# Attention, routed experts and a dense layer in one kernel: one group's preparation a chunk later, a gate split in two, and two small moves

## The chip, the cores and the metric

The kernel runs on one core of a Trainium2 chip. The metric is the device time of one execution in microseconds (us). A core has TensorE (PE in the profile, with its weight loads as PEld), VectorE (DVE), ScalarE (ACT), GpSimd (POOL) and SyncE (SP), which issues most of the DMAs. Each engine takes its own instructions strictly in their order, and waits on semaphores for the others.

## The reference

Three layers in a row, all in float32, on 2304 tokens of width 512:

```
scores = scale * q @ k.T          # 4 x 8 heads, 576 positions, 64 wide
scores = where(0 <= i - j < 64, scores, -1e9);  x = softmax(scores) @ v
logits = x @ w_gate + log1p(exp(x @ w_noise)) * noise
top2   = the two best of 8 experts;  weights = softmax over those two
out[t] = sum over the two of  weight * (relu(x[t] @ w1[e]) @ w2[e])      # 512 -> 1024 -> 512
h = out @ w_in                                                          # 512 -> 2048
g = h if h >= 1;  0 if h <= -1;  else (h + 1)**2 / 4
result = g @ w_out                                                      # 2048 -> 512
```

## The kernel before

The work is one instruction stream per engine, in an order that the program writes out by hand: there is no planner, so an instruction stands where the Python code emits it. Every float32 matrix product is done as three products of rounded parts (high by high, low by high, high by low), so each activation and each weight is split into a high part (a copy on ACT into the rounded type) and a low part (a subtraction on DVE).

The stages around the change, in order of time:

- **Expert 0.** Attention ends; the tokens of expert 0 are worked as unit `0a` (three blocks of 128 rows) and unit `0b` (two). Each unit runs over 8 chunks of the hidden width: `mm1` makes 128 hidden columns for all rows, `act_relu` (lines 892 to 897) takes them out of PSUM as high part (ACT) and low part (DVE), both in the tile `hall`, and `mm2` multiplies them by the second weights. `mm1` of the next chunk is emitted before `mm2` of this one. While `0a` runs, the rest of the routing (`tail`) is fed in as a Python generator, one piece at each `more()`, twice per chunk: once ahead of `mm1`, once behind it. `count` (line 811) is a part of it: it sorts the experts by load and fills `rank_i`, the tables by which the later experts gather their rows, with two products and two reductions on DVE (lines 841 and 845).
- **Expert 1** has six blocks, the sixth of 64 rows. During `0b` each block is gathered, transposed by TensorE into a PSUM bank, and taken out by ACT (high) and DVE (low) in `xpose`. All six blocks use the same bank, number 7 (`TR`), and the last two are turned at the same place of the program, ahead of the last-but-one `mm2` of `0b`.
- **The dense layer** comes after expert 7, whose last unit is `7b`. Its first group of rows, `g0` (two blocks, 256 rows), is worked plainly: 8 chunks `p`, each with two gate halves `f`, in `plain(ui, p)`. For each `f`, 12 matmuls fill bank 0 or 1 (in turn), and `act_gate` computes the piecewise square: ACT reads the bank (`r`), ACT halves it (`m`), two DVE instructions, ACT writes the high part and DVE the low part into `hall`. Then come the 12 matmuls of `mm2`: six of `f=0`, six of `f=1`; of each three the last one reads the low part.
- **The second group**, `g1` (four blocks), and the ones behind it use a Winograd-like scheme with seven products for eight, from `wino(ui, p)`. Its rows have to be ready before that: for each block the two expert results are loaded from DRAM (`y`, on the POOL queue, behind the scatters of unit `7b` into the same DRAM tensor), mixed by the routing weights (`mix_two`, ACT then DVE), turned by TensorE (`xturn`), copied by ACT (`xcopy`), combined (`xsums`, DVE), and split into high and low (`split_two`). All that is placed in the chunks of `g0`: by the table `FILL` into the middle of a gate, and by conditions in the last loop behind a seventh of an `mm2`. `plain(p + 1)` is emitted at the start of step `p`, ahead of that step's `mm2`. At step 6 the first `wino` of `g1` is interleaved with the `mm2` of `g0`; its seven products use bank 0 and bank 1 in turn, and the first one is taken out by ACT (`sg`).

Of the kernel before, what the change touches and what calls it, by code (L numbers as in the profile page):

```python
# [31 lines left out]
NB = 5  # L32
# [25 lines left out]
def fused_kernel(ctx, tc, qT, kT, v, wg, noise, wcat, out, wd=None):  # L58
# [734 lines left out]
    def tail():  # L793
        while live or oq or pq:
            place()
            advance(TAIL)
            yield
        finish_ids([(NA, NB), (0, NA), (NB, E * JB)])
        prep_gather(units[1], 0)
        count()  # L800
        rte.close()
        pool["xp"] = xpc.enter_context(tc.tile_pool(name="xp", bufs=1, reuse_waits="tile", side="right"))
        for n in range(NF, NF + 2):
            load_raw(n)
        yield
        for b in range(1, units[1]["nb"]):
            prep_gather(units[1], b)
            yield
        prep_gather(units[2], 0)

    def count():
        cnt = bank[6][:, CNT:CNT + E]
        nc.tensor.matmul(cnt, lhsT=ones, rhs=state["C"], start=True, stop=True)


        cn = gp.tile([P, E], F32, tag="cn", name="cn")
        key = gp.tile([P, E], F32, tag="key", name="key")
        nc.vector.tensor_scalar(out=cn, in0=cnt, scalar1=16.0, scalar2=None, op0=ALU.mult)
        nc.vector.tensor_tensor(out=key, in0=cn, in1=io8, op=ALU.add)
        nc.vector.memset(key[:, 0:1], -1.0)  # L820
        c8 = gp.tile([P, E], F32, tag="c8", name="c8")
        i8 = gp.tile([P, E], U32, tag="i8", name="i8")
        nc.vector.max(out=c8, in_=key)
        nc.vector.max_index(out=i8, in_max=c8, in_values=key)
        nc.vector.tensor_scalar(out=cnt_i[:, 1:1 + E], in0=i8, scalar1=float(NF), scalar2=None, op0=ALU.mult)
        tf = gp.tile([P, E], F32, tag="tf", name="tf")
        nc.vector.tensor_copy(tf, i8)
        nc.vector.tensor_copy(c8[:, E - 1:E], cn[:, 0:1])
        nc.vector.tensor_tensor(out=c8, in0=c8, in1=caps, op=ALU.subtract)
        nc.vector.tensor_tensor(out=c8[:, 0:E - 1], in0=c8[:, 0:E - 1], in1=tf[:, 0:E - 1], op=ALU.subtract)  # L830
        m1 = gp.tile([P, 1], F32, tag="m1", name="m1")
        nc.vector.tensor_reduce(out=m1, in_=c8, axis=AX.X, op=ALU.max)
        nc.vector.tensor_scalar(out=cnt_i[:, 0:1], in0=m1, scalar1=0.0, scalar2=None, op0=ALU.max)
        R, J = E - 1, NB + 1
        o = gp.tile([P, R, E], F32, tag="to", name="to")
        nc.vector.tensor_tensor(out=o, in0=io8.unsqueeze(1).to_broadcast([P, R, E]),
                                in1=tf[:, 0:R].unsqueeze(2).to_broadcast([P, R, E]), op=ALU.is_equal)
        for a, src in enumerate((src_i, dst_i)):
            f = wk.tile([P, 512], F32, tag="pt", name=f"rk{a}", bufs=PTB)[:, 0:R * J * E]
            f = f.rearrange("p (r j e) -> p r j e", j=J, e=E)  # L840
            nc.vector.tensor_tensor(
                out=f, in0=o.unsqueeze(2).to_broadcast([P, R, J, E]),
                in1=src.rearrange("p (e j) -> p j e", j=JB)[:, 0:J, :].unsqueeze(1).to_broadcast([P, R, J, E]),
                op=ALU.mult)
            nc.vector.tensor_reduce(out=rank_i[:, a], in_=f, axis=AX.X, op=ALU.max)
# [46 lines left out]
    def act_relu(ps, hh, hl, w):  # L892
        nc.scalar.activation(hh, ps, AF.Relu)  # L893
        for o, t in hl:
            c = slice(o, o + t.shape[1])
            nc.vector.scalar_tensor_tensor(out=t, in0=ps[:, c], scalar=0.0, in1=hh[:, c].bitcast(F32), op0=ALU.max,  # L896
                                           op1=ALU.subtract)

    def act_gate(ps, hh, hl, w):
        (_, hl), = hl  # L900
        r = pool["sc"].tile([P, 512], F32, tag="s", name="r")[:, 0:w]
        m = pool["sc"].tile([P, 512], F32, tag="s", name="m")[:, 0:w]
        nc.scalar.activation(r, ps, AF.Relu, bias=1.0)  # L903
        nc.scalar.activation(m, r, AF.Copy, scale=0.5)  # L904
        nc.vector.scalar_tensor_tensor(out=r, in0=m, scalar=1.0, in1=r, op0=ALU.min, op1=ALU.subtract)  # L905
        nc.vector.scalar_tensor_tensor(out=r, in0=m, scalar=1.0, in1=r, op0=ALU.min, op1=ALU.mult)  # L906
        for x in parts_of:
            next(x)
        nc.scalar.activation(hh, r, AF.Copy, scale=-1.0)  # L909
        nc.vector.scalar_tensor_tensor(out=hl, in0=r, scalar=-1.0, in1=hh.bitcast(F32), op0=ALU.mult, op1=ALU.subtract)  # L910
        for x in parts_of:
            next(x, None)
        parts_of.clear()
# [203 lines left out]
    def plain(ui, p):  # L1117
        w = wi[p % WS]
        for f in range(2):
            n = N2 + 2 * p + f  # L1120

            def part(h):
                return [w[:, 2 * f + k // 2, h, P * (k % 2):P * (k % 2) + P] for k in range(4)]
            key = units[ui]["key"]
            parts_of.extend(x() for x in FILL.get((p, f), ()))
            mm1_of(key, n, units[ui]["T"], act_gate, units[ui]["m1"], part(0), part(1))
        load_in(p + WS)

    xops, cs, hs = {}, {}, {}
# [125 lines left out]
        for _ in split_two(ui, j):  # L1255
            pass

    def copy_two(ui, b):
        xcopy(ui, b)
        yield  # L1260

    def sums_two(ui, part):
        yield
        xsums(ui, part)


    SPLITS = {0: [int(F0 <= f < F0 + NF - EW) for f in range(NF)], 1: [0] + [1] * (NF - 1),
              U7A: [1] + [0] * (NF - 1)}
# [12 lines left out]
    for s in range(len(seq)):  # L1281
# [41 lines left out]
        def ahead_xpose():  # L1323
            for x, b, w in ahead:
                if f == (turn_at[b] if ui == WIDE - 1 else w + 2):
                    prep_xpose(x, b, bank[0] if ui == WIDE else TR)
        for x, b, w in ahead:
            if f == w + 1 and x["e"] is None:
                fill.append(lambda x=x, b=b: prep_mix(x, b))
# [45 lines left out]
        if ui == U7B and f:  # L1375
# [3 lines left out]
    assert ndec == n64 and nsplit == nload == N2  # L1379

    AT = ({(4, 0): (None,), (4, 4): (0,), (4, 5): (1,), (5, 0): (2,), (5, 1): (3,), (5, 3): (4,), (6, 2): (5,), (6, 3): (6,)},
          {(5, 3): (6,)})
    g1 = FIRST2 + 1

    def later(fn, *a):
        return lambda: fn(*a)
    FILL.update({(2, 1): [later(mix_two, units[g1], b) for b in (0, 1)],
                 (3, 0): [later(mix_two, units[g1], b) for b in (2, 3)],
                 (4, 0): [later(split_two, g1, 0), later(split_two, g1, 1)],
                 (4, 1): [later(sums_two, g1, (0, 1))],  # L1390
                 (5, 0): [later(sums_two, g1, (2, 3))],
                 (5, 1): [later(split_two, g1, j) for j in (2, 3)],
                 (6, 0): [later(split_two, g1, j) for j in (4, 5)]})
    ndone = 1
    for q, (ui, p) in enumerate(items):
        if q == 0:
# [21 lines left out]
        for j in range(7):  # L1418
            if nxt:
# [6 lines left out]
                if not late:  # L1426
                    if 1 <= p < 3 and j in (2, 4):
                        prep_mix(nxt, 2 * (p - 1) + j // 2 - 1)
                    if 2 <= p < 4 and j in (1, 3):
                        xturn(ui + 1, 2 * (p - 2) + j // 2)  # L1430
                        xcopy(ui + 1, 2 * (p - 2) + j // 2)
                elif p == 2:
                    if j in (0, 1, 5, 6):
                        xturn(ui + 1, j if j < 2 else j - 3)
                    for b in {3: (0, 1), 6: (2, 3)}.get(j, ()):
                        xcopy(ui + 1, b)
                for x in AT[late].get((p, j), ()):
                    xsums(ui + 1) if x is None else xsplit(ui + 1, x)
            if j < len(g):
# [38 lines left out]
```

## Time and profile before

| what | value |
|---|---|
| time, median of 3 runs (range) | 971.39 us (968.99 to 973.98) |
| time of the profiled execution | 971.69 us |
| its span, first to last instruction | 969.9 us |
| TensorE busy | 944.0 us (97%) |
| VectorE / ScalarE / GpSimd busy | 661.6 / 447.5 / 220.2 us |
| mean granted clock of TensorE | 0.994 of full speed |

The profiled execution is 0.3 us above the median. TensorE is busy nearly all the time, so a change can gain only where TensorE stands still or runs at its lower clock; the other engines have idle time of their own that costs nothing.

### The profile page before, as it was taken

How to read it: one execution, taken by the hardware profiler on the slowest of the kernel's cores; microseconds unless marked ns; L12 is line 12 of the kernel's file. 1: busy time of each engine (PE TensorE's matmuls, PEld its weight loads, DVE VectorE, ACT ScalarE, POOL GpSimd, SP SyncE). 2: the span in 40 equal slices, each digit the busy share in tenths (PEclk: the TensorE clock that was granted, in tenths of full speed). 3: DMA queues.
4: the chain of work that ended last, by engine and by line, in shares of the span. 5: the costliest groups of instructions: out<-in, count | busy, mean ns of one | idle time of the engine just before them, and what ended most of it. 6: DMA issues, size and time to landing. Idle time of an engine off the chain costs nothing. (4 is left out here: it accounts for less than half of the span.)

```text
span 969.9 us, 18052 instructions
## 1 busy us (share of the span) xinstructions
PE 944.0 (97%) x6781; PEld 834.8 (86%) x6781; DVE 661.6 (68%) x1388; ACT 447.5 (46%) x920; POOL 220.2 (23%) x273
## 2 busy tenths in 40 slices
PE   8998999999999999999999997999999999999998
PEld 6886878988898989889888886898999889889897
DVE  4689565378997968889543365766766677577664
ACT  6897324345555555555432355334334333443222
POOL 3221113132634354254402130013002201300000
PEclk9999999999999999999999998999999999999999
DMA  8874125445878878757727574684576558546531
GB/s 249 296 266 144 56 97 187 178 167 192 291 257 290 260 244 278 254 196 251 252 82 239 178 234 159 200 298 155 174 249 230 173 174 295 165 161 214 189 106 44
DMA packets 91274, 196.95 MB, mean 203 GB/s; under 512 B 7320, under 2 KB 18072, under 8 KB 91184
## 3 DMA queue, kind: packets, MB, share of 16 engines
q1 hardware_dynamic: 83152, 171.68, 53.6%
q0 software_dynamic: 6736, 21.86, 6.3%
q10 hardware_dynamic: 1296, 2.23, 0.6%
q8 instruction: 54, 0.88, 0.4%
q14 instruction: 36, 0.29, 0.1%
HBM read 155.45 MB, written 40.29 MB: 202 GB/s over the span
## 5 line engine op out<-in xcount | busy, mean ns | idle before, releaser
L949 PE MATMUL bank<-wo,hall 128*128 128x512 f32 x864 | 239.5, 396 | 0.0
L949 PE MATMUL bank<-w,hall 128*128 128x512 f32 (+3 forms) x944 | 236.0, 398 | 1.4 <-DVE hall L896 1.3
L949 PEld LDWEIGHTS bank<-w,hall 128*128 128x128 f32 (+3 forms) x944 | 168.4, 184 | 37.0 <-DVE hall L896 1.7
L949 PEld LDWEIGHTS bank<-wo,hall 128*128 128x128 f32 x864 | 147.8, 190 | 17.5
L893 ACT ACTIVATE hall<-bank 128x288 fp32r<-128x288 f32 (+6 forms) x128 | 54.0, 422 | 223.3 <-PE bank L885 204.1
L885 PE MATMUL bank<-xhie,w 128*128 128x288 f32 (+4 forms) x768 | 123.0, 302 | 1.6 <-DVE hall L896 1.5
L885 PEld LDWEIGHTS bank<-xhie,w 128*128 128x128 f32 x768 | 113.9, 189 | 9.1 <-DVE hall L896 3.4
L896 DVE SCALAR_TENSOR_TENSOR hall<-bank,hall 128x288 fp32r<-128x288 f32 (+7 forms) x168 | 59.8, 391 | 87.2 <-ACT hall L893 78.5
L149 DVE TENSOR_TENSOR w<-raw,w 128x1024 fp32r<-128x1024 f32 (+1 forms) x71 | 82.4, 1160 | 24.4 <-ACT w L158 20.5
L1163 PEld LDWEIGHTS bank<-xb,wi 128*128 128x128 f32 x576 | 80.4, 188 | 11.5 <-DVE wg L1148 1.2
L1187 ACT ACTIVATE hall<-cg 128x512 fp32r<-128x512 f32 x64 | 40.3, 629 | 100.5 <-DVE cg L1185 100.5
L1163 PE MATMUL bank<-xb,wi 128*128 128x256 f32 x576 | 84.8, 283 | 1.8 <-ACT r L903 0.8
L1163 PEld LDWEIGHTS bank<-xc,wi 128*128 128x128 f32 x480 | 67.2, 188 | 7.6 <-DVE wg L1148 0.6
L1030 POOL TENSOR_TENSOR y<-y,y 128x512 f32<-128x512 f32 x14 | 19.1, 1363 | 227.2 <-ACT y L1029 227.2
L1163 PE MATMUL bank<-xc,wi 128*128 128x256 f32 x480 | 70.2, 281 | 0.2
L158 ACT ACTIVATE w<-raw 128x1024 fp32r<-128x1024 f32 (+1 forms) x71 | 69.3, 976 | 0.0
L885 PE MATMUL bank<-xloe,w 128*128 128x288 f32 (+4 forms) x384 | 69.0, 301 | 0.0
L204 POOL TENSOR_TENSOR td<-rawd 128x512 f32<-128x512 f32 x32 | 33.3, 1039 | 140.7 <-DVE rawd L202 78.2
L1181 ACT ACTIVATE mg<-cg 128x512 f32<-128x512 f32 x64 | 40.1, 626 | 47.1 <-DVE cg L1153 45.4
L1182 DVE SCALAR_TENSOR_TENSOR cg<-mg,cg 128x512 f32<-128x512 f32 x64 | 47.0, 734 | 18.8 <-ACT mg L1181 18.8
L885 PEld LDWEIGHTS bank<-xloe,w 128*128 128x128 f32 x384 | 58.0, 188 | 0.0
L1191 DVE SCALAR_TENSOR_TENSOR hall<-cg,hall 128x512 fp32r<-128x512 f32 x64 | 45.9, 718 | 9.1 <-ACT hall L1187 8.7
(279 smaller groups left out, 1443.5 us busy)
## 6 DMA issues: line engine op xcount, KB each, us to landing
wi<-w1o SPq DMA_DIRECT2D x56, 1024.0 KB
raw<-wcat SPq DMA_DIRECT2D x64, 512.0 KB
rawd<-wd SPq DMA_DIRECT2D x32, 512.0 KB
w1o<-so SPq DMA_DIRECT2D x64, 256.0 KB
y<-y_dram SPq DMA_DIRECT2D x28, 256.0 KB
vE<-v SPq DMA_DIRECT2D x18, 260.0 KB
x_dram<-x SPq DMA_DIRECT2D x18, 256.0 KB
k<-kT SPq DMA_DIRECT2D x8, 512.0 KB
```

The lines of the kernel that those rows point to most:

```text
L149: nc.vector.tensor_tensor(out=w[:, 1, c], in0=t[:, c], in1=w[:, 0, c].bitcast(F32), op=ALU.subtract)
L158: nc.scalar.activation(w[:, 0, c], t[:, c], AF.Copy)
L204: nc.gpsimd.tensor_tensor(out=t, in0=hf, in1=lf, op=ALU.add)
L885: nc.tensor.matmul(ps, lhsT=l[k], rhs=r[:, k, s:s + w], start=(c == 0), stop=(c == len(prods) - 1))
L893: nc.scalar.activation(hh, ps, AF.Relu)
L896: nc.vector.scalar_tensor_tensor(out=t, in0=ps[:, c], scalar=0.0, in1=hh[:, c].bitcast(F32), op0=ALU.max, op1=ALU.subtract)
L949: nc.tensor.matmul(M2[b][0:w], lhsT=h2[:, o:o + w], rhs=r[n], start=(first and a == 0), stop=(last and a == end))
L1163: nc.tensor.matmul(ps, lhsT=w[:, l, k * P:k * P + P], rhs=r[:, m, k, :], start=(c == 0), stop=(c == len(prods) - 1))
L1181: nc.scalar.activation(st["m"], c, AF.Relu, scale=0.5)
L1182: nc.vector.scalar_tensor_tensor(out=c, in0=st["m"], scalar=1.0, in1=c, op0=ALU.min, op1=ALU.subtract)
L1187: nc.scalar.activation(h2[:, 0:T], c, AF.Copy, scale=-1.0)
L1191: nc.vector.scalar_tensor_tensor(out=h2[:, T:2 * T], in0=c, scalar=-1.0, in1=h2[:, 0:T].bitcast(F32), op0=ALU.mult, op1=ALU.subtract)
```

## The change

Five edits:

1. `count` gets a `yield` ahead of the two rank tables, and `tail` passes it on with `yield from`, so that the tables and what follows are emitted one `more()` later.
2. `act_gate` no longer finishes its own gate. It keeps `(r, hh, hl)` in `held_gate`, and the next gate finishes it (`close_gate`) right behind its own read of the bank. The last gate is closed at the end of the last `plain`.
3. The sixth block of expert 1 is turned into bank 4 instead of bank 7.
4. The preparation of `g1` moves back: the mixing of blocks 0 and 1 by one gate or two, the turns from step 2 to steps 3 and 4, copies, sums and splits accordingly. The sums leave the gate and stand in step 4; the last split goes into the last plain chunk.
5. Two helpers that are no longer used are removed.

```
-        count()
+        yield from count()
...
+        yield
         for a, src in enumerate((src_i, dst_i)):
...
+    held_gate = []
+
+    def close_gate():
+        for r, hh, hl in held_gate:
+            nc.scalar.activation(hh, r, AF.Copy, scale=-1.0)
+            nc.vector.scalar_tensor_tensor(out=hl, in0=r, scalar=-1.0, in1=hh.bitcast(F32), op0=ALU.mult,
+                                           op1=ALU.subtract)
+        held_gate.clear()
+
     def act_gate(ps, hh, hl, w):
...
         nc.scalar.activation(r, ps, AF.Relu, bias=1.0)
+        close_gate()
         nc.scalar.activation(m, r, AF.Copy, scale=0.5)
...
+        held_gate.append((r, hh, hl))
         for x in parts_of:
             next(x)
-        nc.scalar.activation(hh, r, AF.Copy, scale=-1.0)
-        nc.vector.scalar_tensor_tensor(out=hl, in0=r, scalar=-1.0, in1=hh.bitcast(F32), op0=ALU.mult, op1=ALU.subtract)
...
+        if p == NPR - 1:
+            close_gate()
...
-                    prep_xpose(x, b, bank[0] if ui == WIDE else TR)
+                    prep_xpose(x, b, bank[0] if ui == WIDE else bank[4] if ui == WIDE - 1 and b == NB else TR)
...
-          {(5, 3): (6,)})
+          {})
+    TURN, COPY = {(3, 0): (0,), (3, 1): (1,), (3, 6): (2,), (4, 0): (3,)}, {(3, 3): (0, 1), (4, 2): (2, 3)}
...
-    FILL.update({(2, 1): [later(mix_two, units[g1], b) for b in (0, 1)],
-                 (3, 0): [later(mix_two, units[g1], b) for b in (2, 3)],
-                 (4, 0): [later(split_two, g1, 0), later(split_two, g1, 1)],
-                 (4, 1): [later(sums_two, g1, (0, 1))],
-                 (5, 0): [later(sums_two, g1, (2, 3))],
-                 (5, 1): [later(split_two, g1, j) for j in (2, 3)],
-                 (6, 0): [later(split_two, g1, j) for j in (4, 5)]})
+    FILL.update({(3, 0): [later(mix_two, units[g1], 0)],
+                 (3, 1): [later(mix_two, units[g1], 1)],
+                 (4, 0): [later(mix_two, units[g1], b) for b in (2, 3)],
+                 (5, 0): [later(split_two, g1, j) for j in (0, 1)],
+                 (6, 0): [later(split_two, g1, j) for j in (2, 3)],
+                 (6, 1): [later(split_two, g1, j) for j in (4, 5)],
+                 (7, 0): [later(split_two, g1, 6)]})
...
-                elif p == 2:
-                    if j in (0, 1, 5, 6):
-                        xturn(ui + 1, j if j < 2 else j - 3)
-                    for b in {3: (0, 1), 6: (2, 3)}.get(j, ()):
+                else:
+                    for b in TURN.get((p, j), ()):
+                        xturn(ui + 1, b)
+                    for b in COPY.get((p, j), ()):
                         xcopy(ui + 1, b)
+                    if p == 4 and j > 4:
+                        xsums(ui + 1, (0, 1) if j == 5 else (2, 3))
```

On **VectorE, at the end of expert 0's unit `0a`**, this stands in a row before (`rk` and `rank_i` are the rank tables, `hall` the low parts of the ReLUs of the last two chunks of `0a`):

```order
L833 TENSOR_SCALAR cnt_i_194<-m1_2437 128x1
L836 TENSOR_TENSOR to_2440<-io8_177,tf_2432 128x56
L841 TENSOR_TENSOR rk0_2442<-to_2440,src_i_190 128x336
L845 TENSOR_REDUCE rank_i_205<-rk0_2442 128x42
L841 TENSOR_TENSOR rk1_2445<-to_2440,dst_i_191 128x336
L845 TENSOR_REDUCE rank_i_205<-rk1_2445 128x42
L896 SCALAR_TENSOR_TENSOR hall_2150<-bank1_74,hall_2150 128x384
L896 SCALAR_TENSOR_TENSOR hall_2150<-bank2_75,hall_2150 128x384
```

And in the changed kernel, on VectorE at the same place:

```order
L833 TENSOR_SCALAR cnt_i_194<-m1_2437 128x1
L836 TENSOR_TENSOR to_2440<-io8_177,tf_2432 128x56
L842 TENSOR_TENSOR rk0_2451<-to_2440,src_i_190 128x336
L846 TENSOR_REDUCE rank_i_205<-rk0_2451 128x42
L842 TENSOR_TENSOR rk1_2454<-to_2440,dst_i_191 128x336
L846 TENSOR_REDUCE rank_i_205<-rk1_2454 128x42
L897 SCALAR_TENSOR_TENSOR hall_2150<-bank1_74,hall_2150 128x384
L897 SCALAR_TENSOR_TENSOR hall_2150<-bank2_75,hall_2150 128x384
```

Nothing moved there: only the line numbers and a tile's number differ.

On **ScalarE, in the gates of `g0` around the mixing** (`r` and `m` as above, `hall` the high part of a gate, `y2` to `y5` the four blocks of `g1`), before, from the second half of `plain(2)` to the second half of `plain(3)`:

```order
L903 ACTIVATE r_7017<-bank1_74 128x256
L904 ACTIVATE m_7018<-r_7017 128x256
L1019 ACTIVATE y2_6963<-y2_6963,wts_189 128x512
L1019 ACTIVATE y3_6966<-y3_6966,wts_189 128x512
L909 ACTIVATE hall_2150<-r_7017 128x256
L903 ACTIVATE r_7056<-bank0_73 128x256
L904 ACTIVATE m_7057<-r_7056 128x256
L1019 ACTIVATE y4_6970<-y4_6970,wts_189 128x512
L1019 ACTIVATE y5_0_6974<-y5_0_6974,wts_189 128x512
L909 ACTIVATE hall_2150<-r_7056 128x256
```

And now, on ScalarE, from the first half of `plain(3)` to the first half of `plain(4)`:

```order
L913 ACTIVATE r_7050<-bank0_73 128x256
L904 ACTIVATE hall_2150<-r_7015 128x256
L915 ACTIVATE m_7051<-r_7050 128x256
L1029 ACTIVATE y2_6961<-y2_6961,wts_189 128x512
L913 ACTIVATE r_7072<-bank1_74 128x256
L904 ACTIVATE hall_2150<-r_7050 128x256
L915 ACTIVATE m_7073<-r_7072 128x256
L1029 ACTIVATE y3_6964<-y3_6964,wts_189 128x512
L913 ACTIVATE r_7109<-bank0_73 128x256
L904 ACTIVATE hall_2150<-r_7072 128x256
L915 ACTIVATE m_7110<-r_7109 128x256
L1029 ACTIVATE y4_6968<-y4_6968,wts_189 128x512
```

The high part of a gate moved behind the next gate's read, so it no longer stands behind a mix of its own gate; the mixes moved one to two gates later.

On **ScalarE, at the start of the Winograd products** (`xa2` is the last split of `g1`, `sg1_0` the copy of the first product out of bank 0), before:

```order
L1250 ACTIVATE xa2_7175<-xhis_7108 128x512
L903 ACTIVATE r_7321<-bank0_73 128x256
L904 ACTIVATE m_7322<-r_7321 128x256
L909 ACTIVATE hall_2150<-r_7321 128x256
L903 ACTIVATE r_7341<-bank1_74 128x256
L904 ACTIVATE m_7342<-r_7341 128x256
L909 ACTIVATE hall_2150<-r_7341 128x256
L1144 ACTIVATE sg1_0_7365<-bank0_73 128x256
```

And now:

```order
L913 ACTIVATE r_7317<-bank0_73 128x256
L904 ACTIVATE hall_2150<-r_7280 128x256
L915 ACTIVATE m_7318<-r_7317 128x256
L1262 ACTIVATE xa2_7235<-xhis_7159 128x512
L913 ACTIVATE r_7339<-bank1_74 128x256
L904 ACTIVATE hall_2150<-r_7317 128x256
L915 ACTIVATE m_7340<-r_7339 128x256
L904 ACTIVATE hall_2150<-r_7339 128x256
L1156 ACTIVATE sg1_0_7365<-bank0_73 128x256
```

The read of bank 1 moved ahead of the high part of the gate before it; the last high part and `sg1_0` stand in the same order as before, and the split `xa2` now stands between the two reads.

## Rows read from the trace of the kernel before

**Rows 1.** The page: busy time of each engine.

```profile
PE 944.0 (97%) x6781; PEld 834.8 (86%) x6781; DVE 661.6 (68%) x1388; ACT 447.5 (46%) x920; POOL 220.2 (23%) x273
```

**Rows 2.** Waits of PE: engine, line, waited for; us in total, times, longest.

```profile
PE bank L1221 <- DVE y L1021: 5.5, 1, 5.5
...
PE bank L756 <- DVE xloe L760: 1.8, 2, 1.5
...
PE bank L1163 <- ACT r L903: 0.8, 1, 0.8
PE bank L1163 <- ACT sg L1144: 0.6, 1, 0.6
```

**Rows 3.** Windows: length, busy time of each engine, PEclk, DMA share, GB/s.

```profile
140.00:142.00 2.00, 0.73 (x3) 0.29 (x3) 1.97 (x5) 0.79 (x2) 0.95 (x1) 1.00 0.94 305
169.64:173.05 3.41, 3.41 (x10) 2.83 (x11) 1.65 (x2) 1.31 (x2) 0.00 (x0) 0.50 0.11 46
586.07:592.90 6.83, 5.63 (x19) 4.67 (x20) 5.45 (x11) 4.37 (x11) 0.00 (x0) 0.50 0.28 104
```

**Rows 4.** Timeline at the rank tables: start, length, engine, line [idle before <- releaser].

```profile
140.71 0.50 DVE L845 TENSOR_REDUCE rank_i<-rk 128x42 int32<-128x336 f32 x1
...
141.73 1.88 PE L949 MATMUL bank<-w,hall 128*128 128x512 f32 x7 [1.27 <-DVE hall L896]
```

**Rows 5.** Timeline at expert 1's last two blocks.

```profile
167.17 0.46 PE L756 MATMUL bank<-idr,xge 128*128 128x128 f32 x4
...
168.33 0.69 DVE L760 TENSOR_TENSOR xloe<-bank,xhie 128x512 fp32r<-128x512 f32 x1
...
169.08 0.50 PE L756 MATMUL bank<-idr,xge 64*128 64x64 f32 x4 [1.46 <-DVE xloe L760]
```

**Rows 6.** Timeline at the first chunk of `g0`.

```profile
569.47 1.99 ACT L1111 ACTIVATE wo<-wr 128x1024 fp32r<-128x1024 f32 x2
...
570.54 2.36 DVE L1112 TENSOR_TENSOR wo<-wr,wo 128x1024 fp32r<-128x1024 f32 x2 [0.27 <-ACT wo L1111]
```

**Rows 7.** Timeline from `mm2` of step 1 to `plain(4)`.

```profile
576.00 2.91 PE L949 MATMUL bank<-wo,hall 128*128 128x512 f32 x12
576.22 0.37 ACT L903 ACTIVATE r<-bank 128x256 f32<-128x256 f32 x1
...
578.44 0.42 DVE L910 SCALAR_TENSOR_TENSOR hall<-r,hall 128x256 fp32r<-128x256 f32 x1 [0.49 <-ACT hall L909]
...
578.74 1.11 PE L885 MATMUL bank<-xhig,wi 128*128 128x256 f32 x8
...
581.61 0.72 ACT L1019 ACTIVATE y<-y,wts 128x512 f32<-128x512 f32 x1 [2.48 <-DMA y<-y_dram]
...
585.06 0.72 ACT L1019 ACTIVATE y<-y,wts 128x512 f32<-128x512 f32 x1 [2.73 <-DMA y<-y_dram]
...
587.26 1.12 PE L1221 MATMUL bank<-idn,y 128*128 128x128 f32 x4 [5.53 <-DVE y L1021]
...
594.48 1.07 PE L885 MATMUL bank<-xhig,wi 128*128 128x256 f32 x8
```

**Rows 8.** Timeline: four float32 transposes without a stall, and what follows them.

```profile
560.27 0.60 PE L756 MATMUL bank<-idn,y 128*128 128x128 f32 x4
...
560.63 2.08 PE L949 MATMUL bank<-w,hall 128*128 128x512 f32 x8
```

**Rows 9.** Timeline at the first Winograd products.

```profile
613.95 0.89 PE L1163 MATMUL bank<-xb,wi 128*128 128x256 f32 x6
...
615.85 0.97 PE L1163 MATMUL bank<-xb,wi 128*128 128x256 f32 x6 [0.79 <-ACT r L903]
...
617.19 0.42 ACT L909 ACTIVATE hall<-r 128x256 fp32r<-128x256 f32 x1 [0.95 <-DVE r L906]
617.51 0.36 ACT L1144 ACTIVATE sg<-bank 128x256 f32<-128x256 f32 x1
...
617.93 0.98 PE L1163 MATMUL bank<-xb,wi 128*128 128x256 f32 x6 [0.64 <-ACT sg L1144]
```

## What I predict, and how it is worked out

> **What bounds the kernel now.** I read four views in this order. The page first: TensorE is busy for 944.0 us of a span of 969.9 us [rows 1], so at most 26 us can come from filling its idle time, and the other engines matter only where TensorE waits for one of them. Then TensorE's waits, summed by line [rows 2]: one wait of 5.5 us, for the mixed rows of the second dense group, is by far the longest; the others that stand near an edit are the sixth block of expert 1 (1.5 us at most), and two short ones where the Winograd products start (0.8 and 0.6 us). Then the windows of lower clock [rows 3]: the granted clock falls to 0.50, the lower of the two levels (1.2 GHz), for 3.41 us from 169.64 and for 6.83 us from 586.07. Both stand right behind the two longest waits. A busy stretch of 3.41 us at half clock does the work of 1.7 us, so the waits cost more than their own length. Last the timeline around each edit, for what releases TensorE there.
>
> The profiled execution took 971.69 us, 1.8 us more than its span; I make the sum against it. It stands 0.3 us above the median of the runs shown, whose spread is 5 us.
>
> **The rank tables: no change.** The low part of the ReLU stands on VectorE behind four instructions of the tables, and TensorE waits 1.27 us for it [rows 4]. The order excerpt shows the same eight instructions in the same row in the changed kernel: the piece behind the new `yield` is taken up at the next `more()`, and that one stands ahead of the next `mm1`, so no ReLU is emitted in between. The matmuls in between are TensorE's and don't move against VectorE. I take 0. The ends are 0 and minus 1.27, since no instruction is added.
>
> **The sixth block: minus 3.2 us.** The transposes of the fifth block start at 167.17; those of the sixth follow at 169.08, after 1.46 us of waiting until VectorE has emptied bank 7, in an instruction that began at 168.33 and takes 0.69 [rows 5]. With bank 4 this wait goes: the bank's last user was the unit before. What is late next is the sixth block's own low part, which VectorE makes behind the fifth's, from 169.02 on. The next `mm1` needs it only in its second half of rows, behind six matmuls of `mm2`; about 0.2 us at most is lost if it waits with its first. The lower clock that follows the wait costs 1.7 us [rows 3], and I take it to go with the wait: minus 1.46, minus 1.7.
>
> That the clock falls because of a wait this short is read from one place. The wait of 1.27 us at 140.46 was not followed by a fall: the window around it shows 1.00 [rows 3, 4]. The Trainium skill ("TensorE: Matmul & The Clock Gate", section "HAM oscillation — how this bites in real kernels") warns only of idle gaps well longer than 1.46 us. By that rule the fall at 169.64 had another cause and stays, and the sum would be 1.7 us smaller. The row speaks against the rule, as the fall begins 0.6 us behind the wait; I keep the row, and the rule as a rival.
>
> **The second group's rows: minus 8.6 us.** TensorE stood still from 581.73 (587.26 less 5.53), and the next `plain` started at 594.48 [rows 7]: 12.75 us. The work in it is the 12 matmuls of one `mm2`, which take 2.74 us without a stall (576.00 to 578.74, [rows 7]), and four times four transposes, 0.36 us each four (560.27 to 560.63, [rows 8]), 1.44 together. The rest, 8.57 us, is the stall and the lower clock behind it, and it is what can be won.
>
> What made the stall: ScalarE waited for the second block's load until 585.06, and the high part of the gate stood behind this mix in its queue; TensorE's first transposes then came at 587.26 [rows 7]. The loads hang on the scatters of unit `7b` and don't move by the edit. In the new order TensorE has, at 581.73, the `mm2` of step 2 (2.74 us) and the gate matmuls of `plain(4)` ahead of it (578.74 to 581.73: 2.99 us), so it asks for the first mixed block at about 587.4 and for the second at about 588.0 (0.36 and one matmul of 0.23 later). The second block lands at 585.06 and is mixed by ScalarE (0.72) and VectorE (0.75 at most) by 586.6: 1.4 us to spare. The `mm2` of step 2 no longer waits either, since the high part of its second gate now stands ahead of the first mix. Behind the waiting mix stand, on ScalarE, only the read of `plain(4)`'s first bank, which is not full before 586, and the high part of the gate before it, which `mm2` of step 3 needs at about 589. The third and fourth block are mixed one gate later and turned after 590. Nothing in the list is as late as before; I take the whole 8.57. If the loads came 2 us later, 0.6 us would come back; the end of the range on this side is minus 6.
>
> **The gate that is held: plus 0.2 us.** A gate took 2.64 us from its read (576.22) to the end of its low part (578.44 and 0.42, [rows 7]). Now its last two instructions come behind the next gate's read: for a chunk's second gate one `mm2` (2.74), one gate's matmuls (1.5) and about 1.4 us of finishing after its own matmuls, 5.6 us. Its low part is wanted by the third matmul of the second half of its `mm2`: 2.74 and 2.99 us, half an `mm2` (1.37) and two matmuls (0.46), 7.6 us. That leaves 2.0 us in every chunk. Only in the first chunk two long subtractions for the output weights stand between (2.36 us of VectorE, from 570.54, behind 1.99 us of ScalarE, [rows 6]): the low part falls from before them to behind them. In exchange ScalarE loses the pause it made for the gate, about 1.4 us, so the subtractions start that much earlier and end near 571.6; the low part is there at 572.1, and TensorE wants it at 572.0. I take plus 0.2; the ends are minus 0.2 and, if the subtractions don't move up, plus 1.3.
>
> **The start of the Winograd products: 0.** Between 613.95 and 617.93 two waits of 0.79 and 0.64 us stand [rows 9]. The first was for the read of bank 1, and it goes: this read no longer stands behind the high part before it. The second was for `sg`, the copy out of bank 0, and in the new order it still stands behind the last gate's high part, which still waits for its two VectorE instructions; in front of it stand now the last split (the order excerpt), and on VectorE the splits of the gate before. I count from the second gate's matmuls: 0.4 us until ScalarE reads, the read 0.37, the other gate's high part 0.42, `m` 0.42, two VectorE instructions 0.86, high part 0.42, `sg` 0.36, and hand-offs of 0.1 us each: about 3.8 us, against 3.98 before. So two waits become one of about 1.7 us. The ends are minus 1.4 (both gone) and plus 1 (VectorE is further behind).
>
> Sum: 0 - 3.2 - 8.6 + 0.2 + 0 = -11.6; 971.7 - 11.6 = 960.1. **Forecast: 960 us.**
>
> **Rivals.**
>
> *The clock falls elsewhere.* The one wait of about 1.7 us at the Winograd start is longer than the 1.46 us that had a fall behind it, so the clock can fall there: plus 1.7, 961.8. By the skill's rule as weighed above the fall behind the sixth block stays: also 961.8. Each is open; both together 963.5. For it: the fall at 169.64. Against: the two waits at the Winograd start, 1.43 us in one stretch of 4 us, had none behind them.
>
> *The wait for the rows only shrinks.* The loads could land later, since all transfers crowd here. If the second block lands 4 us later than 585.06, TensorE waits 2.6 us, and the clock falls behind it for 1.7 or 3.4: 964.4 to 966.1. Against: the transfers that stand beside them are issued behind the same gate matmuls as before.
>
> *Slower: the held gate is late in each chunk.* If finishing a gate took longer than the 2.0 us to spare, all seven chunks that have a successor would wait at the second half of their `mm2`. It decides from 3.7 us too late on: then each waits 1.7 us, 11.9 together, and the kernel is at 972 or above. Against: a whole gate takes 2.64 us, and each chunk of ScalarE has six instructions of some 0.4 us in 5.7 us of TensorE.
>
> *The tables do get out of the way:* minus 1.27, 958.8. The order speaks against it.
>
> **How the numbers follow.** Forecast as worked out, 958.5 to 961.5: 0.50. The clock falls in one place or two, 961.5 to 964: 0.22. The wait only shrinks, 964 to 968: 0.10, half of it still more than 0.5% faster. Better than the forecast, by the tables or by both waits at the Winograd start, 957 to 958.5: 0.08. The held gate is late: 0.05, of which 0.03 slower by more than 0.5%. Something else that eats the gain: 0.05. A change of 0.5% (4.9 us) is about what a measurement of this kernel can tell from none: faster means under 966.5. From the cases: 0.50 + 0.22 + 0.05 + 0.08 = 0.85 and a little of the last two, 0.87 faster; 0.08 the same; 0.05 slower. The range leaves out the slow end of the last three cases and the best of the fourth: 957.3 to 965.
>
> **What the changed profile would show.** No wait for `y` among TensorE's waits, and no lower clock in the chunks of `g0`; the transposes of block 0 and 1 right behind `plain(4)`. The transposes of the sixth block within 0.5 us of the fifth's, and a clock of 1.00 behind them. Still 1.3 us of waiting behind the rank tables. One wait of 1.3 to 2.3 us for `sg`. I am wrong if ScalarE still waits for a load while TensorE stands, if the waits behind held gates come to more than 2 us, or if the lower clock returns behind a wait under 1.5 us.

## The result, and the profile after

| what | before | after |
|---|---|---|
| time, median of 6 runs each (range) | 971.14 us (968.99 to 973.98) | 958.91 us (958.29 to 960.74) |
| ratio, with its 95% interval | 1 | 0.9878 (0.9860 to 0.9896) |
| span of the profiled execution | 969.9 us | 956.5 us |
| TensorE busy | 944.0 us | 939.3 us |
| mean granted clock | 0.994 | 0.999 |

The changed kernel is 12.2 us faster; 11.6 were forecast. The line of the page that answers to [rows 1]:

```profile
PE 939.3 (98%) x6781; PEld 831.6 (87%) x6781; DVE 660.5 (69%) x1388; ACT 444.8 (46%) x920; POOL 219.9 (23%) x273
```

TensorE does the same 6781 matmuls in 4.7 us less, because they no longer run at half clock anywhere behind the edits (3.41 us, and 5.63 busy of 6.83 us, before); the other 8.7 us of the span are idle time that went. Of TensorE's waits, the lines that answer to [rows 2] (engine, line, waited for; us in total, times, longest):

```profile
PE bank L959 <- DVE hall L897: 1.3, 1, 1.3
...
PE bank L1175 <- ACT sg L1156: 0.9, 1, 0.9
```

The wait for `y` (5.5), the one for `xloe` (1.8) and the one for `r` (0.8) are gone from the list; of the 1.8, 0.3 belong to an earlier block of expert 1. The 1.3 us behind the rank tables are still there, and the wait for `sg` grew from 0.6 to 0.9. The windows that answer to [rows 3] (length, busy time of each engine, PEclk, DMA share, GB/s):

```profile
140.00:142.00 2.00, 0.84 (x4) 0.71 (x5) 1.97 (x5) 0.20 (x1) 0.94 (x1) 1.00 0.93 352
169.00:173.00 4.00, 4.00 (x26) 3.86 (x25) 1.29 (x3) 0.93 (x2) 0.00 (x0) 1.00 0.42 140
585.00:592.00 7.00, 7.00 (x48) 6.34 (x48) 3.69 (x10) 4.16 (x12) 0.00 (x0) 1.00 0.43 146
```

The granted clock is 1.00 (2.4 GHz) in all three, and TensorE is busy all through the second and the third.

**The rank tables** in the timeline (start, length, engine, line [idle before <- releaser]), as in [rows 4]:

```profile
140.13 0.50 DVE L846 TENSOR_REDUCE rank_i<-rk 128x42 int32<-128x336 f32 x1
...
141.16 1.89 PE L959 MATMUL bank<-w,hall 128*128 128x512 f32 x7 [1.29 <-DVE hall L897]
```

Nothing changed: 1.29 us for 1.27.

**Expert 1's last blocks**, as in [rows 5]:

```profile
166.08 0.89 PE L756 MATMUL bank<-idr,xge 128*128 128x128 f32 x8
...
166.90 1.65 PE L959 MATMUL bank<-w,hall 128*128 128x512 f32 x6
...
167.25 1.02 DVE L760 TENSOR_TENSOR xloe<-bank,xhie 128x512 fp32r<-128x512 f32 x2
```

The two blocks' transposes are one piece of eight now. Both low parts end at 168.27; the first matmul that reads such rows comes later, so it waits for nothing. A row of matmuls of expert 1 behind this place, in the kernel before and then in the changed one:

```profile
174.49 1.44 PE L885 MATMUL bank<-xhie,w 128*128 128x352 f32 x8
```

```profile
170.31 1.44 PE L886 MATMUL bank<-xhie,w 128*128 128x352 f32 x8
```

**The chunks of `g0`**, as in [rows 7]:

```profile
574.37 1.11 PE L886 MATMUL bank<-xhig,wi 128*128 128x256 f32 x8
...
578.19 0.73 ACT L1029 ACTIVATE y<-y,wts 128x512 f32<-128x512 f32 x1 [1.21 <-DMA y<-y_dram]
...
579.96 1.11 PE L886 MATMUL bank<-xhig,wi 128*128 128x256 f32 x8
...
582.79 0.60 PE L1233 MATMUL bank<-idn,y 128*128 128x128 f32 x4
...
583.46 0.60 PE L1233 MATMUL bank<-idn,y 128*128 128x128 f32 x4
...
592.88 1.11 PE L886 MATMUL bank<-xhig,wi 128*128 128x256 f32 x8
```

The same matmul can be followed through both traces. The gate matmuls of `plain(3)` that stood at 578.74 before stand at 574.37 (4.37 us earlier); the next chunk, `plain(4)`, moved from 594.48 to 579.96 (14.52), because the transposes have not been paid yet; two chunks on, at `plain(6)`, with all four blocks turned in both, 605.53 became 592.88: 12.65 us earlier. The row of the kernel before:

```profile
605.53 1.11 PE L885 MATMUL bank<-xhig,wi 128*128 128x256 f32 x8
```

The stretch gave 12.65 - 4.37 = 8.3 us. ScalarE still waits for a load, 1.21 us, but with nothing of TensorE behind it.

**The Winograd start**, as in [rows 9]:

```profile
601.29 0.89 PE L1175 MATMUL bank<-xb,wi 128*128 128x256 f32 x6
601.49 0.38 ACT L913 ACTIVATE r<-bank 128x256 f32<-128x256 f32 x1
...
602.06 0.42 ACT L904 ACTIVATE hall<-r 128x256 fp32r<-128x256 f32 x1 [0.18 <-DVE r L917]
...
602.38 0.40 ACT L915 ACTIVATE m<-r 128x256 f32<-128x256 f32 x1
...
603.79 0.42 ACT L904 ACTIVATE hall<-r 128x256 fp32r<-128x256 f32 x1 [1.01 <-DVE r L917]
604.11 0.36 ACT L1156 ACTIVATE sg<-bank 128x256 f32<-128x256 f32 x1
...
604.53 0.98 PE L1175 MATMUL bank<-xb,wi 128*128 128x256 f32 x6 [0.93 <-ACT sg L1156]
```

From the first product to the third it is 3.24 us (601.29 to 604.53), where it was 3.98.

Stage by stage, the edits are thus worth 3.1 us at the sixth block (the same matmuls 1.09 earlier ahead of it, 4.18 behind it), 0.3 in the first chunks of `g0`, 8.3 in the moved preparation and 0.7 at the Winograd start: 12.4. The two spans differ by 13.4; the other 1.0 lies ahead of the sixth block, 0.6 in attention and the rest at a wait of unit `0b` (0.32 us, at 157.60 in the kernel before) that the traces of experiments 2 and 3, which have the kernel before at that place, do not show; it is not the change's.

### The profile page after: what moved, and what is told of

Same layout as the page of the kernel before. It is cut to its first block, busy times and chain, and to the rows that moved or that the text cites. A ratio compares the mean times of both kernels' runs of the same rounds, so it can differ in the third digit from the quotient of the medians.

```text
span 956.5 us, 18052 instructions
## 1 busy us (share of the span) xinstructions
PE 939.3 (98%) x6781; PEld 831.6 (87%) x6781; DVE 660.5 (69%) x1388; ACT 444.8 (46%) x920; POOL 219.9 (23%) x273
```

## The experiments

Each was run beside the kernel before, which took 971.03 us beside experiments 1, 2, 4 and 5, 970.18 beside 3, 8, 9 and 10, and 968.78 beside 6, 7, 11 and 12. Differences of about 1 us between experiments of different groups are therefore not shown by their times; the ratios to the kernel before and the traces have to say it.

**1. The sixth block in bank 7 again**, the rest as in the changed kernel.

```
-  prep_xpose(x, b, bank[0] if ui == WIDE else bank[4] if ui == WIDE - 1 and b == NB else TR)
+  prep_xpose(x, b, bank[0] if ui == WIDE else TR)
```

> The changed kernel with the sixth block of expert 1 put back into bank 7. My account: the wait of 1.46 us ahead of the sixth block's transposes is back, the clock falls to 0.50 for 3.4 us behind it, and the kernel takes 3.1 us more than the changed one: 962.0 us. Rival (a wait this short does not move the clock, the fall had another cause): the wait alone, 1.5 us more, 960.4, and the clock stays at 1.00 around it.

Measured: 962.04 us (960.02 to 963.44), 3.1 more than the changed kernel. The transposes in the timeline, then the window behind them:

```profile
169.04 0.50 PE L756 MATMUL bank<-idr,xge 64*128 64x64 f32 x4 [1.46 <-DVE xloe L760]
```

```profile
169.91:173.32 3.41, 3.41 (x12) 2.92 (x11) 1.65 (x2) 0.99 (x2) 0.00 (x0) 0.50 0.10 20
```

The wait is back, and the half clock (1.2 GHz) for 3.41 us: 1.46 + 1.7 = 3.2; the trace has 3.1 in the stage. The account holds for the traced execution.

It does not hold for all of them. The mean granted clock was 0.997 to 0.998 in three of the six executions (962.19 to 963.44 us) and 0.999 to 1.000 in the other three (960.02 to 961.88 us). A fall of 3.41 us takes 3.41 x 0.5 / 961.7 = 0.0018 off the mean, so the second three had none. The account describes one half of the executions and the rival the other, and the median lies between them.

**2. The kernel before with that wait filled.** Six 128x512 matmuls into bank 4, their result thrown away, between the fifth and the sixth block's transposes.

```
+  if ui == WIDE - 1 and b == NB:
+      for _ in range(6):
+          nc.tensor.matmul(bank[4], lhsT=whi[n][:, 0:P], rhs=vhi[n], start=True, stop=True)
```

> The kernel before, with six matmuls of 128x512 (0.24 us each) added between the transposes of the fifth and the sixth block, into bank 4, which nobody reads; they fill the wait of 1.46 us with work that is thrown away. My account (the fall of the clock follows from the idle time): the clock stays at 1.00 behind 169 us, and the kernel takes 1.7 us less than before: 969.4 us, though it does more. Rival (the clock falls for another reason): no gain, 971.1, and 0.50 in the same place.

Measured: 969.77 us against 971.03, ratio 0.9989 (0.9977 to 1.0002); the times alone can't tell 1.3 us from none. The trace can. Timeline, then window:

```profile
168.14 1.60 PE L1328 MATMUL bank<-w 128*128 128x512 f32 x6
169.76 0.50 PE L756 MATMUL bank<-idr,xge 64*128 64x64 f32 x4
```

```profile
169.00:173.00 4.00, 3.98 (x23) 3.21 (x22) 2.34 (x3) 1.33 (x2) 0.00 (x0) 1.00 0.39 131
```

The sixth block is turned no sooner, and yet the clock stays at 1.00, and the stage is 1.6 us shorter than before. One execution without a fall would not be enough (experiment 1), but the mean clocks agree: none of the 12 executions is under 0.996, while 10 of the 17 of the kernel before beside them are at 0.994 or 0.995, as its trace with both falls is. So this fall follows from TensorE's idle time, not from the place.

**3. The long wait of the kernel before filled** in the same way, with 22 matmuls ahead of the first transposes of `g1`.

```
+  if ui == FIRST2 + 1 and b == 0:
+      for _ in range(22):
+          nc.tensor.matmul(to, lhsT=idr, rhs=vhi[N2 + 4], start=True, stop=True)
```

> The kernel before, with 22 matmuls of 128x512 added ahead of the first turned block of the second dense group, into bank 7, which the transposes then overwrite; they fill the wait of 5.5 us with work that is thrown away. My account: the wait itself is not shortened, since it ends with the mixed rows, but the clock does not fall for 6.8 us behind it, of which 5.6 were busy: 2.8 us less than before, 968.3 us. Rival: the load of the rows, not the wait, lowers the clock, or the added matmuls delay the transposes as much as they save: 971.1 us.

Measured: 968.89 us against 970.18, ratio 0.9985 (0.9971 to 0.9999). Timeline, then window:

```profile
582.80 5.19 PE L1222 MATMUL bank<-wo,idr 128*128 128x512 f32 x22
587.84 0.60 PE L1224 MATMUL bank<-idn,y 128*128 128x128 f32 x4
```

```profile
586.00:593.00 7.00, 7.00 (x43) 5.98 (x42) 5.42 (x11) 4.40 (x11) 0.00 (x0) 1.00 0.51 193
```

No fall. Followed by the same matmuls as above (`plain(3)` at 579.98, `plain(6)` at 603.53), this stretch costs 5.0 us more than the changed kernel's (5.61 us late ahead of it, 10.65 behind it), where that of the kernel before costs 8.3: some 3.2 us of the term were clock, and 5.0 were the wait. The mean clock is at 0.997 or above in 11 of the 12 executions; the kernel before beside them is never above 0.996.

**4. The held gate and bank 4 alone**, with the preparation of `g1` where it was before (tables `FILL`, `TURN` and the conditions of step 2 as in the kernel before).

> The changed kernel with the second dense group's mixes, turns, copies, sums and splits put back where they were; held gate and bank 4 stay. My account: the placing made the whole gain of this stage and the held gate has no part in it, so TensorE waits for the mixed rows again and 8.3 us come back: 967.2 us. Rival: the held gate alone already frees the low part of the first mixed block from standing behind a high part, so the stall is only some 3.5 us and its low clock 2 us: 964.4 us.

Measured: 964.24 us (961.82 to 966.57); the rival was right. The first mix and its turn in the timeline, and the window behind:

```profile
582.19 0.72 ACT L1028 ACTIVATE y<-y,wts 128x512 f32<-128x512 f32 x1 [5.12 <-DMA y<-y_dram]
582.95 0.75 DVE L1030 SCALAR_TENSOR_TENSOR y<-y,wts 128x512 f32<-128x512 f32 x1 [4.93 <-ACT y L1028]
...
583.75 1.09 PE L1232 MATMUL bank<-idn,y 128*128 128x128 f32 x4 [2.42 <-DVE y L1030]
```

```profile
583.82:587.23 3.41, 3.41 (x12) 2.75 (x13) 2.60 (x5) 2.60 (x6) 0.00 (x0) 0.50 1.03 383
```

With the mixes unmoved the wait falls from 5.5 to 2.4 us, and the half clock from 6.83 to 3.41 us. Before, the first block was loaded at 581.61 and turned at 587.26 [rows 7]; here it is turned 1.56 us after its load. The timeline of the kernel before shows the detour in between:

```profile
585.69 0.40 ACT L909 ACTIVATE hall<-r 128x256 fp32r<-128x256 f32 x1
...
586.12 0.43 DVE L910 SCALAR_TENSOR_TENSOR hall<-r,hall 128x256 fp32r<-128x256 f32 x1 [6.07 <-ACT hall L909]
...
586.46 1.41 DVE L1021 SCALAR_TENSOR_TENSOR y<-y,wts 128x512 f32<-128x512 f32 x2
```

On ScalarE the gate's high part came behind the second block's mix, which waited for its load until 585.06; on VectorE the gate's low part, which needs that high part, stood ahead of the first block's mix. With the held gate neither stands there. What the stretch still loses against the changed kernel is 8.35 - 3.97 = 4.4 us (`plain(3)` at 578.34, `plain(6)` at 601.23), so the held gate by itself wins 3.9 of the 8.3 us in this trace.

**5. The moves and bank 4 alone**, with the old gate.

```
-  close_gate()                      # behind the read
-  held_gate.append((r, hh, hl))
+  nc.scalar.activation(hh, r, AF.Copy, scale=-1.0)
+  nc.vector.scalar_tensor_tensor(out=hl, in0=r, scalar=-1.0, in1=hh.bitcast(F32), ...)
```

> The changed kernel with the old gate, which finishes itself; new placing and bank 4 stay. My account: the gate matters only where a bank is read, 0.35 us in the first chunk and 0.74 us at the first Winograd products: 960.0 us, and no wait for the mixed rows. Rival: without the held gate a high part stands behind a mix that waits for its load, and TensorE waits 3 us or more in the middle of the group: 962 us or above.

Measured: 963.26 us (961.66 to 965.50). Neither was right: the rival's time came, but no wait for `y`. The stretch of the moved preparation is as short as in the changed kernel:

```profile
576.97 1.11 PE L886 MATMUL bank<-xhig,wi 128*128 128x256 f32 x8
...
595.48 1.11 PE L886 MATMUL bank<-xhig,wi 128*128 128x256 f32 x8
```

From `plain(3)` to `plain(6)` it is 18.51 us, and 18.51 in the changed kernel (574.37 to 592.88): the moves win the whole 8.3 us without the held gate. And yet the trace is 5.0 us longer. Of these, 0.2 stand in the first chunks (the read of bank 1), 2.4 at the Winograd start, and 2.4 lie ahead of `g0`, where the two programs are the same; that those follow from the edit is not shown. At the Winograd start the timeline has:

```profile
604.36 1.29 DVE L1253 TENSOR_TENSOR xa<-xlos,xa 128x512 fp32r<-128x512 f32 x2
...
606.48 0.42 ACT L910 ACTIVATE hall<-r 128x256 fp32r<-128x256 f32 x1 [1.25 <-DVE r L907]
606.80 0.36 ACT L904 ACTIVATE r<-bank 128x256 f32<-128x256 f32 x1
...
607.22 0.98 PE L1164 MATMUL bank<-xb,wi 128*128 128x256 f32 x6 [1.71 <-ACT r L904]
```

The moved splits put two long subtractions of VectorE ahead of the gate. In the old order ScalarE waits for VectorE in the gate (`hall`) before it reads the next bank (`r`), and TensorE waits for this read. The held gate reads first. So the later placing pays in full only with the held gate.

**6. One subtraction less ahead of that gate.** Experiment 5 with the fourth split one chunk earlier.

```
-  (6, 0): [later(split_two, g1, j) for j in (2, 3)],
-  (6, 1): [later(split_two, g1, j) for j in (4, 5)],
+  (6, 0): [later(split_two, g1, j) for j in (2, 3, 4)],
+  (6, 1): [later(split_two, g1, 5)],
```

> The changed kernel with the old order in the small group's gate, and with its fourth split of rows one chunk earlier, so that one xa subtraction of VectorE instead of two stands ahead of the last chunk's first gate. Theory (VectorE's subtractions hold that gate and with it the read of the second bank): the 1.71 us wait of TensorE for that read shrinks by the half of it that a 0.64 us subtraction makes, to about 1.1 us, and the time is 962.6 us. Rival (ScalarE's own order holds the read): the wait stays at 1.7 us and the time at 963.3 us.

Measured: 962.48 us (960.37 to 965.81). The timeline at the first products and a window:

```profile
606.80 0.98 PE L1164 MATMUL bank<-xb,wi 128*128 128x256 f32 x6 [0.83 <-ACT r L904]
...
609.10 1.38 PE L1164 MATMUL bank<-xb,wi 128*128 128x256 f32 x6 [1.09 <-ACT r L904]
```

```profile
608.00:612.00 4.00, 2.84 (x12) 2.11 (x11) 2.88 (x7) 1.79 (x5) 0.00 (x0) 0.68 0.58 223
```

The second wait fell from 1.71 to 1.09 us as the theory said, but the first grew from 0.26 to 0.83: together 1.92 us for 1.97. The wait moved with the subtraction, which shows that VectorE's queue holds the read; nothing was won by it. The times say the same: 0.9926 of the kernel before here, 0.9927 in experiment 5, so that 962.48 lies near the 962.6 of the theory is luck. And here the clock fell behind the second wait, which it did not in the trace with the 1.71.

**7. The wait of 1.46 us, later by seven matmuls.** The length of a wait does not tell by itself whether the clock falls, so this run of the kernel before keeps the length and moves the place.

```
+  if ui == WIDE - 1 and f == 1:
+      for _ in range(7):
+          nc.tensor.matmul(bank[4], lhsT=whi[n][:, 0:P], rhs=vhi[n], start=True, stop=True)
```

> The kernel before with seven 128x512 matmuls (about 1.7 us, thrown away, into bank 4) in the second chunk of unit 0b's rows, so that the 1.46 us wait ahead of the sixth block comes 1.7 us later with the same length. Theory (not the length of a wait alone decides, but also where it falls; the 1.71 us wait at the Winograd start in the run with the old gate left the clock at 1.00): the clock stays at 1.00 behind this wait, and what the seven cost is given back, 971.1 us. Rival (each wait of 1.46 us has a fall of 3.41 us behind it): the clock falls to 0.50 behind it again, 972.8 us.

Measured: 970.32 us against 968.78, ratio 1.0010 (0.9997 to 1.0023). Timeline, then window:

```profile
170.38 0.50 PE L756 MATMUL bank<-idr,xge 64*128 64x64 f32 x4 [1.46 <-DVE xloe L760]
```

```profile
172.00:173.80 1.80, 1.80 (x6) 1.45 (x5) 1.23 (x1) 0.24 (x1) 0.00 (x0) 0.50 0.00 0
```

The clock fell again: my theory of the place fell with it. The run is 1.5 us longer than the kernel before beside it, where the rival said 1.7; the rival's 972.8 was counted from another run of the kernel before, at 971.1.

**8. The rank tables out of the way**, with a second `yield` ahead of the tables.

> The changed kernel with a second yield ahead of the rank tables, which puts them behind the ReLU of the last chunk but one on VectorE. My account: the wait of 1.29 us for this ReLU goes, but the low parts of the next unit's rows now stand behind the tables, and about 0.6 us of waiting comes in front of their first matmuls: 958.2 us. Rival (the tables are not what holds the ReLU up, but the chain of small routing instructions ahead of them): no change, 958.9.

Measured: 958.63 us (957.40 to 958.94), 0.9875 of the kernel before, where the changed kernel had 0.9878: no difference in the times. In the trace the wait of 1.29 us is gone, but the rows of `0b` are late by 0.55 instead, and 1.0 us is left of 1.6 in the stage.

**9. Tables and the gather that needs them behind the rows of `0b`.**

> The changed kernel with the two rank tables and the first gather of expert 1 moved behind the rows of unit 0b on VectorE (their scratch then lies in another pool). My account: no wait for the ReLU and none for the rows; the first gather starts some 3 us later, which its first use 14 us on does not feel: 1.3 us less than the changed kernel, 957.6. Rival: the first block's gather is late for its transposes, and the gain is lost: 958.9 or more.

Measured: 958.31 us (957.82 to 958.89), 0.9873 of the kernel before: again no difference that the times can show. The whole 1.6 us stays in the stage; at the end of unit `7b`, where TensorE waits for rows of `g0` that DRAM delivers, 0.7 of it is lost.

**10. Experiment 9, and the last gate closed behind `sg`** (the `close_gate()` at the end of the last `plain` moves behind the first product's gate).

> The changed kernel with the tables last, and with the last plain gate finished only behind the copy sg of the first Winograd product. My account: 1.3 us from the tables, and the wait of 0.93 us for sg goes as well, because the copy then stands ahead of the high part: 956.7 us. Rival: the read of bank 1 by VectorE, or the gate's low part, is the next to be late at the Winograd start, and only the tables' part is won: 957.6.

Measured: 957.07 us (956.17 to 957.50). At the Winograd start:

```profile
602.07 0.36 ACT L1158 ACTIVATE sg<-bank 128x256 f32<-128x256 f32 x1
...
602.83 0.87 PE L1177 MATMUL bank<-xb,wi 128*128 128x256 f32 x6
```

TensorE no longer waits for `sg`; the stage is 0.6 us shorter. (The "silu half" of the next expectation is this copy `sg`.)

**11 and 12. The changed kernel and experiment 10 again, side by side.**

> The changed kernel once more, as the measure for the others of this call: 958.9 us by either account.

> The changed kernel with the rank tables and the first transposed read behind unit 0b's rows, and with the last plain gate closed behind the silu half of the first Winograd product's gate. Account: the 1.29 us wait of the tables (1.3 to 1.6 us in their stage) and the 0.6 us at the Winograd start stay saved to the end, 2.0 to 2.2 us less than the changed kernel of this call, about 956.8 us. Rival: attention behind the tables gives most of it back, since its units start earlier and find less ready, and the difference is under 1 us.

Measured: 958.69 us (957.96 to 961.42) and 957.22 us (956.68 to 957.70). The difference of 1.5 us lies between the two expectations: in the trace 1.6 and 0.6 us are gained in their stages, and 1.0 is lost where `g0`'s rows are turned, as 0.7 was in experiment 9. That the edit causes this loss is not shown: the trace of experiment 10, the same program, has no such wait, and that of experiment 5, without these edits, has one of 0.5 us. This is the fastest version, 0.9876 of the kernel before (0.9858 to 0.9895).

## Why the prediction was right, and where it was not

- **The bound.** Right: what was gained was TensorE's idle time and half clock at the places that the waits and the clock windows showed. One reading was loose: the second stretch of half clock does not stand "right behind" its wait, but begins at 586.07, 1.2 us before the wait ended at 587.26.
- **Rank tables, 0.** Right; the order had shown it, and experiments 8 and 9 show what moving them is worth (at most 1.6 in the stage; at the end too little for the times to show).
- **Sixth block, minus 3.2.** Measured 3.1 in the trace, and 3.1 by undoing it. The rival that the fall stays is refuted: it goes with the wait (experiment 2), and it came with the wait in the traces of 1 and 7. But the sum took the fall for certain behind such a wait, and by the mean clocks of experiment 1 it came in three executions of six: the 1.7 us are the price of an execution that has it, as the one traced before did. The Trainium skill's rule ("TensorE: Matmul & The Clock Gate", section "HAM oscillation — how this bites in real kernels") warns of much longer gaps only, and does not account for the falls of experiments 1, 4 and 7 behind waits of 1.46 and 2.42 us; the measurements decide.
- **Second group's rows, minus 8.6.** Measured 8.3, and the moves alone win all of it (experiment 5). The held gate alone wins 3.9 of it (experiment 4): the two don't add, since each takes away a link of the same chain. The prediction had seen that the high part of the gate "stood behind this mix", and not that VectorE's first mix stood behind that in turn; so it took the held gate for a cost alone ("plus 0.2"). Nor did it say that the moves need the held gate: without it they lose 2.4 us at the Winograd start. The sum came out because it was made of the stall as a whole, with both edits in.
- **Held gate, plus 0.2.** Measured 0.05 lost in the first chunk and 0.35 won where bank 1 is read in the next: minus 0.3. No later chunk waits for a held gate, so the rival by which each of them does is out.
- **Winograd start, 0.** This is the term that was mis-sized: minus 0.7. The form was right, two waits into one for `sg`, but 0.9 us long and not 1.7. The chain was counted at 3.8 us with each ScalarE instruction at its length plus a hand-off, 0.5 us. The rows above show neighbours on ScalarE that don't need each other's results starting 0.32 us apart (602.06 and 602.38, 603.79 and 604.11), and the read coming 0.2 us after the matmuls and not 0.4. That is the 0.6 us. [Rows 9] had the same step: 617.19 and 617.51.
- **The sum.** The errors of the terms partly cancel: the first two gains were put 0.1 and 0.3 us too high, the last two 0.5 and 0.7 too low. That the total lies within 1 us is in part luck.
- **The clock falls elsewhere.** It did not in the trace of the changed kernel, whose wait there was 0.9 us. Of its 12 executions (experiment 11 included) three have a mean clock of 0.997 or 0.998, so a fall somewhere; where is not shown. In the traces of experiments 4, 6 and 10 it fell in attention, outside the edits.

## What to carry to other kernels

When one stall has several links in a row (a late load, an instruction that stands behind whoever waits for it, a third that needs that instruction), two edits can each take away a link, and their gains don't add: here 8.3 us and 3.9, together 8.3. Price the stall as a whole, run each edit alone before giving either the credit, and follow it to the end of the kernel, where an edit alone can lose what it won. An engine that finishes its old work behind the next read, and not ahead of it, hands the producer its buffer back without waiting for a third engine. Read hand-offs within one engine as the distance between two starts in the trace, not as a length plus a gap.

## What was not expected of the hardware

Waits of about the same length did and did not have a fall of the clock behind them. In the traces the granted clock fell to 0.50 for 3.41 us behind 1.46 us (experiments 1 and 7), and within 4 us of the pair 0.83 and 1.09 us (experiment 6); it stayed at 1.00 behind 1.27 to 1.29 us at the rank tables, and in experiment 5 through 0.26, 1.71 and 0.86 us in a row:

```profile
604.00:608.00 4.00, 2.04 (x14) 1.67 (x14) 3.46 (x8) 2.30 (x6) 0.00 (x0) 1.00 0.62 218
608.00:612.00 4.00, 3.14 (x22) 2.57 (x21) 2.19 (x6) 0.69 (x2) 0.00 (x0) 1.00 0.12 45
```

TensorE was busy for half of the first window and kept its clock. Neither the length of a wait nor its place in the program decides alone, since executions of one and the same kernel differ: by the mean clock three of six had no fall in experiment 1, and three of six none in experiment 4 (1.000, at 961.82 to 963.74 us), whose trace has one behind 2.42 us; two of six had some fall in experiment 5 (0.997), whose trace has none. Only one execution of each was traced, so the waits of the others are not shown. What decides is left open. What was shown is that work in the wait, even thrown away, keeps the clock up (experiments 2 and 3), and that a fall cost about 1.6 us per 3.41 (1.6 in experiment 2, 3.2 for 6.83 in experiment 3). To see whether a fall belongs to a kernel or to one execution, look at the mean clock of all its runs beside the trace.
